# First weight tiles converted inside the attention prologue, and a new order of the two weight matrices

## The chip, the cores and the metric

The kernel runs on one core of one Trainium2 chip. The metric is the device time of one execution in microseconds (us), lower is better. Engines are named as in the profile: PE (matmul, with PEld for its weight loads), DVE (VectorE), ACT (ScalarE), POOL (GpSimd) and SP (SyncE, which only issues transfers here).

## The reference, cut to what matters

Three stages follow each other: a decaying linear attention, a feed-forward block with softplus, and a second one with a clipped gate. The weights come as float64 and all results are float32.

```python
for t in range(S):                                   # B=2, H=8, S=768, D=64
    state = gamma[None, :, None, None] * state + np.einsum('bhd,bhe->bhde', k[:, :, t], v[:, :, t])
    y[:, :, t] = scale * np.einsum('bhd,bhde->bhe', q[:, :, t], state)
x = y.transpose(0, 2, 1, 3).reshape(B * S, H * D)    # 1536 x 512
h = x @ w_in                                         # 512 x 2048
x = (np.maximum(h, 0.0) + np.log1p(np.exp(-np.abs(h)))) @ w_out
h = x @ w2_in
out = (h * np.clip(h + 3.0, 0.0, 6.0) / 6.0) @ w2_out
```

## The kernel before

**Attention** is cut into 12 units of 128 positions (two batches of six). For a unit `u`, `prepare` transposes k and q on PE and copies them out on ACT (`kT`, `qT`), and scales v (`vs`); `scores` multiplies them on PE and DVE masks the result into `pt`; `carry` multiplies q with the running state `bd` on PE, after which POOL fades `bd`; `intra` multiplies `pt` with `vs` on PE, DVE scales the sum into `on`, ACT copies it to `x_hi` and POOL subtracts to get `x_lo`; `state` adds to `bd` on DVE. Four units fill one chunk of 512 rows of x.

**The feed-forward blocks** run over three chunks of 512 rows and 16 slices `f` of the hidden width. One step is `gemm1` (12 matmuls of 128x512 on `x_hi`, `x_lo` and the two parts of a tile of w_in, then `g`, `e`, `hi` and `lo` on ACT and DVE) and, two steps later, `gemm2` (12 matmuls with a tile of w_out). Each product of float32 numbers is made of three products of shorter parts, high and low.

**Weights** arrive as pairs of 32-bit words. `fetch` loads a tile of 512 KB into one of three `raw` buffers by SP. `convert` makes the high and the low part: ACT scales the upper word, DVE clamps (`raw<-raw`), shifts (`w<-raw`) and joins in two operations of three operands (`w<-raw,w`), ACT copies out the high part, and the low part is `w` minus the high part. In the first eight conversions that subtraction is a POOL instruction (`w_parts<-w,w_parts`); in the later ones it is an accumulating transfer issued by POOL (`w_parts<-w`). The list `order` says which tile comes when: `EARLY` = 4 tiles of w_in, then w_out and w_in by turns. `feed(n)` converts up to the n-th tile; `first(f)` is the n that is called for after `gemm1` of step f in the first chunk.

**What sets the order.** While `nc.on` is true, every instruction keeps the order in which it is written, on every engine; this holds for the constants, units 0 to 3 with the preparation of unit 4, and the first two conversions (`feed(2)`, after unit 3). From then on a scheduler places what is written: units 4 to 11 are interleaved with steps 0 to 7 of the first chunk.

Of the kernel before, what the change touches and what calls it, by code (L numbers as in the profile page):

```python
# [10 lines left out]
F32 = mybir.dt.float32  # L11
# [3 lines left out]
ALU = mybir.AluOpType  # L15
# [25 lines left out]
@with_exitstack  # L41
def kernel(ctx, tc, q, k, v, w1_in, w1_out, w2_in, w2_out, tq, tk, tc_, tg, out):
    nc = InOrder(tc)
    B, H, S, D = q.shape
    NT, DM = out.shape
    DFF = w1_in.shape[1]
    NP = H // 2
    KD = DM // P
    NF = DFF // P
    C = P  # L50
    NCH = S // C
    CH = 512
    chunks1 = [(0, 0, 512), (1, 0, 512), (2, 0, 512)]
    chunks2 = [(0, 0, 512), (1, 0, 512), (2, 0, 512)]
    LAG = 2
    EARLY = 4

    tc.nc.scalar.preload_act_table_set("softplus")

    xpool = ctx.enter_context(tc.tile_pool(name="xpool", bufs=1))  # L60
    x_hi = [xpool.tile([P, KD, CH], F32R, name=f"x_hi{c}") for c in range(NT // CH)]
    x_lo = [xpool.tile([P, KD, CH], F32R, name=f"x_lo{c}") for c in range(NT // CH)]

    win_p = ctx.enter_context(tc.tile_pool(name="win", bufs=NF))
    wout_p = ctx.enter_context(tc.tile_pool(name="wout", bufs=NF))
    psum = ctx.enter_context(tc.tile_pool(name="psum", bufs=1, space=PSUM))
    raw_p = ctx.enter_context(tc.tile_pool(name="raw", bufs=3))
    cv_p = ctx.enter_context(tc.tile_pool(name="cv", bufs=2))

    w_in_t, w_out_t, raws = {}, {}, {}  # L70
    words = {0: (w1_in.bitcast(U32), w1_out.bitcast(U32)), 1: (w2_in.bitcast(U32), w2_out.bitcast(U32))}

    def fetch(m, o, f):
        raw = raw_p.tile([P, CH, 2], U32, tag="raw", name="raw")
        src = words[m][o]
        if o:
            nc.sync.dma_start(out=raw.rearrange("p n t -> p (n t)"), in_=src[f * P:(f + 1) * P, :])
        else:
            nc.sync.dma_start(out=raw.rearrange("p (k n) t -> p k (n t)", k=KD),
                              in_=src[:, 2 * f * P:2 * (f + 1) * P].rearrange("(k p) f -> p k f", p=P))  # L80
        raws[m, o, f] = raw

    def convert(m, o, f):

        raw = raws.pop((m, o, f))
        low, y = raw[:, :, 0], raw[:, :, 1]

        w = cv_p.tile([P, CH], U32, tag="w", name="w")
        nc.scalar.activation(y.bitcast(F32), y.bitcast(F32), AF.Copy, scale=2.0 ** -112)
        nc.vector.tensor_scalar(y.bitcast(F32), y.bitcast(F32), -TOP, TOP, ALU.max, ALU.min)  # L90
        nc.vector.tensor_scalar(w, y, 3, None, ALU.logical_shift_left)
        nc.vector.scalar_tensor_tensor(w, y, 0x80000000, w, ALU.bitwise_and, ALU.bitwise_or)
        nc.vector.scalar_tensor_tensor(w, low, 29, w, ALU.logical_shift_right, ALU.bitwise_or)
        t = (wout_p if o else win_p).tile([P, 2, CH], F32R, tag="w", name="w_parts")
        if done[1] < 2 * EARLY:
            nc.scalar.activation(t[:, 0], w.bitcast(F32), AF.Copy)
            nc.gpsimd.tensor_tensor(t[:, 1], w.bitcast(F32), t[:, 0].bitcast(F32), ALU.subtract)
        else:
            nc.scalar.activation(t[:, 1], w.bitcast(F32), AF.Copy, scale=-1.0)
            nc.gpsimd.dma_start(out=t[:, 1].bitcast(F32), in_=w.bitcast(F32), accum_op=ALU.add)  # L100
            nc.scalar.activation(t[:, 0], w.bitcast(F32), AF.Copy)
        if o:
            w_out_t[m, f] = t
        else:
            w_in_t[m, f] = t.rearrange("p a (k n) -> p a k n", k=KD)

    NU = B * NCH
    order = [(0, 0, f) for f in range(EARLY)]
    for f in range(NF):
        order += [(0, 1, f)] + [(0, 0, f + EARLY)] * (f + EARLY < NF)  # L110
    order += [(1, 0, f) for f in range(NF)] + [(1, 1, f) for f in range(NF)]
    done = [0, 0]

    def fetch_weights(n):
        while done[0] < min(len(order), n):
            fetch(*order[done[0]])
            done[0] += 1

    def feed(n):

        n = min(n, len(order))
        while done[1] < n:
            fetch_weights(done[1] + (1 if nc.on else 2))
            convert(*order[done[1]])
            done[1] += 1

    banks = psum.tile([P, 8, CH], F32, name="banks")
    free = list(range(8))

    def bank(hold=False):  # L130

        i = free.pop(0)
        if not hold:
            free.append(i)
            return banks[:, i, :]
        return i, banks[:, i, :]

    def release(i):
        free.append(i)

    def first(f):
        return EARLY + 2 * (f + 1) - max(0, f + 1 + EARLY - NF)

    step, last, n_steps = moe(ctx, tc, nc, out, x_hi, x_lo, w_in_t, w_out_t, chunks1, chunks2, NF, KD, DM, CH, LAG, feed, first, bank, release)
    s = 0
    with ExitStack() as actx:
        unit = attention(actx, tc, nc, q, k, v, tq, tk, tc_, tg, x_hi, x_lo, CH, bank, feed, fetch_weights)
        for u in range(CH // P, NU):
            begin, end = unit(u)
            begin()  # L150
            step(s, True, False)
            end()
            step(s, False, True)
            s += 1
    while s < n_steps:
        step(s)
        s += 1


def attention(ctx, tc, nc, q, k, v, tq, tk, tcc, tg, x_hi, x_lo, CH, bank, feed, fetch_weights):  # L160
# [4 lines left out]
    START = CH // C  # L165
# [5 lines left out]
    def ps(*shape):  # L171
        return bank().rearrange("p (a b) -> p a b", a=shape[0])
# [14 lines left out]
    def fetch(u, *which, parts=1):  # L187
        b, i = units[u]
        for nm in which:
            t = ld.tile([P, H, D], F32, tag=nm + "0" * (u < START), name=nm, bufs=START if u < START else 3)  # L190
            src = {"q": q, "k": k, "v": v}[nm][b, :, i * C:(i + 1) * C, :].rearrange("h s d -> s h d")
            for j in range(parts):
                hs = slice(j * H // parts, (j + 1) * H // parts)
                nc.sync.dma_start(out=t[:, hs], in_=src[:, hs])
            nat[nm, u] = t
# [27 lines left out]
    def carry(u):  # L223
        b, i = units[u]
        qT = tr["q", u]
        o = ps(NP, C)
        tr["o", u] = o
        if i > 0:
            for p in range(NP):
                nc.tensor.matmul(o[:, p, :], bd[b][:, p, :], qT[:, p, :], start=(p == 0), stop=False, skip_group_check=True)  # L230
        fade(u)

    def intra(u):
        b, i = units[u]
        vs, pt, o = tr["vs", u], tr["pt", u], tr["o", u]
        for h in range(H):
            g = h % 2
            nc.tensor.matmul(o[g * D:(g + 1) * D, h // 2, :], vs[:, h, :], pt[:, g, h // 2, :],
                             start=(i == 0 and h < 2), stop=True, skip_group_check=True)
        c, at = divmod(u * C, CH)  # L240
        hi, lo = x_hi[c][:, :, at:at + C], x_lo[c][:, :, at:at + C]
        on = wk.tile([P, NP, C], F32, tag="on" + "0" * (u < START), name="on", bufs=2)
        nc.vector.tensor_tensor(on, o, tq_sb, ALU.mult)
        nc.scalar.activation(hi, on, AF.Copy)
        nc.gpsimd.tensor_tensor(lo, on, hi.bitcast(F32), ALU.subtract)
# [18 lines left out]
    def fade(u):  # L264
        b, i = units[u]
        if i == 0 or i == NCH - 1:
            return
        for j in range(2):
            r = slice(j * D, (j + 1) * D)
            s = bd[b][r, :, r]  # L270
            nc.gpsimd.tensor_tensor(s, s, tc_sb[r].rearrange("p (n o) -> p n o", o=1).to_broadcast([D, NP, D]), ALU.mult)
# [12 lines left out]
    fetch(1, "v")  # L284
    for u in range(2, START):
        fetch(u, "k", "q", "v")
    fetch_weights(1)
    fetch(START, "k", "q", "v")

    def prepare(u):  # L290
        transposed(u, "k")
        transposed(u, "q")
        decayed(u)
# [9 lines left out]
    for u in range(START):  # L303
        scores(u)
        prepare(u + 1)
        carry(u)
        intra(u)
        state(u)
    feed(2)
    nc.on = False  # L310
    for u in range(START + 1, START + 3):
        fetch(u, "k", "q", "v")

    def unit(u):

# [146 lines left out]
```

## Time and profile before

| | before |
|---|---|
| median of 3 timed runs | 617.2 us (616.24 to 618.05) |
| span of the profiled execution, first to last instruction | 613.8 us |
| PE busy | 598.1 us, 97% |
| DVE busy | 351.8 us, 57% |
| ACT busy | 275.9 us, 45% |
| POOL busy | 103.4 us, 17% |

The page gives no time of the profiled execution other than its span; the timed runs lie 2.4 to 4.3 us above that span. The averages hide two stages: in the first 160 us attention, weights and the first chunk overlap and DVE is full; in most of the rest PE alone is full. So the table is read together with windows of the trace.

### The profile page before, as it was taken

The page shows a single profiled execution, that of the slowest core. Times are in us where ns is not written, and L with a number is a line of the kernel's source. Part 1 is how long each engine was busy: PE and PEld are TensorE (multiplying, and loading weights), DVE is VectorE, ACT ScalarE, POOL GpSimd, SP SyncE. Part 2 cuts the span into 40 slices and gives each one's busy share as a digit, 9 for nine tenths or more (in the row PEclk, how much of TensorE's full clock was granted, in tenths as well). Part 3 has the DMA queues.
Part 4 walks back from the last instruction along what each step waited for, and adds up shares of the span by engine and source line. Part 5 has one row for each costly group of instructions (what it writes and reads, how often), then busy time and mean ns, then how long its engine had stood idle before and what let it go on. Part 6 is the DMA issues. An engine that isn't in the chain of part 4 may idle for free.

```text
span 613.8 us, 7743 instructions
## 1 busy us (share of the span) xinstructions
PE 598.1 (97%) x2963; PEld 491.2 (80%) x2963; DVE 351.8 (57%) x583; ACT 275.9 (45%) x473; POOL 103.4 (17%) x110
## 2 busy tenths in 40 slices
PE   7988999999999999999999999999999999999997
PEld 6865778788788888888887878888888888888886
DVE  4589999999773334376667798832322222322223
ACT  3355475678563333465556687722222222222220
POOL 1745664432100000011111122200000000000000
PEclk9998999999999999999999999999999999999999
DMA  9998888799600000045566689600100000100001
GB/s 193 236 229 211 219 197 208 192 217 227 159 32 0 1 0 1 9 111 119 140 180 154 162 208 262 125 7 1 68 1 0 1 1 0 70 1 1 0 1 69
DMA packets 69510, 61.60 MB, mean 100 GB/s; under 512 B 40032, under 2 KB 56672, under 8 KB 69472
## 3 DMA queue, kind: packets, MB, share of 16 engines
q1 hardware_dynamic: 61408, 46.42, 26.6%
q0 software_dynamic: 8064, 14.68, 14.6%
q8 instruction: 23, 0.38, 0.3%
q14 instruction: 15, 0.12, 0.1%
HBM read 43.26 MB, written 3.15 MB: 76 GB/s over the span
## 4 chain that ended last, share of the span: by engine, by line
PE 66%; DVE 13%; issue 7%; DMA 6%; ACT 3%; POOL 2%; SPq 1%; DVEq 0%; POOLq 0%; ACTq 0%
PE banks L31 66%; DVE w L31 6%; DMA raw<-in_moe_w_in_dram 3%; DVE raw L31 2%; POOL w_parts L31 2%; DMA w_parts<-w 2%; DVE g L31 1%; SPq L31 1%; DVE pt L31 1%; DMA q<-in_q_dram 1%; DVE lo L31 1%; ACT e L31 1%; DVE e L31 1%; ACT raw L31 1%; ACT w_parts L31 1%
## 5 line engine op out<-in xcount | busy, mean ns | idle before, releaser
L31 PE MATMUL banks<-x_hi,w_parts 128*128 128x512 f32 x768 | 253.9, 391 | 2.4 <-POOL w_parts L31 1.2
L31 PEld LDWEIGHTS banks<-x_hi,w_parts 128*128 128x128 f32 x768 | 143.8, 188 | 34.4 <-POOL w_parts L31 2.1
L31 PE MATMUL banks<-x_lo,w_parts 128*128 128x512 f32 x384 | 149.6, 390 | 0.0
L31 PE MATMUL banks<-hi,w_parts 128*128 128x512 f32 x384 | 129.4, 397 | 0.9 <-POOL w_parts L31 0.8
L31 PE MATMUL banks<-w_parts,hi 128*128 128x512 f32 (+1 forms) x386 | 118.4, 388 | 0.7 <-DVE g L31 0.7
L31 DVE SCALAR_TENSOR_TENSOR g<-e,banks 128x512 f32<-128x512 f32 x48 | 33.0, 687 | 123.3 <-ACT e L31 123.3
L31 DVE SCALAR_TENSOR_TENSOR w<-raw,w 128x512 uint32<-128x512 uint32 x128 | 94.3, 738 | 1.6
L31 DVE TENSOR_TENSOR lo<-g,hi 128x512 fp32r<-128x512 f32 x96 | 66.3, 690 | 48.9 <-ACT hi L31 48.6
L31 POOL DMA_DIRECT2D w_parts<-w x56 | 49.3, 880 | 251.9 <-DVE e L31 98.7
L31 ACT ACTIVATE hi<-g 128x512 fp32r<-128x512 f32 x96 | 60.5, 630 | 65.0 <-DVE g L31 61.6
L31 ACT ACTIVATE e<-banks,three 128x512 f32<-128x512 f32 x48 | 32.9, 686 | 125.7 <-PE banks L31 125.7
L31 ACT ACTIVATE w_parts<-w 128x512 fp32r<-128x512 f32 x120 | 70.4, 625 | 39.2 <-DVE w L31 39.0
L31 PEld LDWEIGHTS banks<-hi,w_parts 128*128 128x128 f32 x384 | 72.8, 190 | 17.6 <-POOL w_parts L31 1.5
L31 PEld LDWEIGHTS banks<-w_parts,hi 128*128 128x128 f32 x386 | 72.3, 188 | 16.0 <-DVE g L31 1.1
L31 PEld LDWEIGHTS banks<-x_lo,w_parts 128*128 128x128 f32 x384 | 72.1, 188 | 14.9
L31 PE MATMUL banks<-lo,w_parts 128*128 128x512 f32 x192 | 75.6, 394 | 0.4 <-DVE lo L31 0.4
L31 PE MATMUL banks<-w_parts,lo 128*128 128x512 f32 (+1 forms) x193 | 74.9, 388 | 0.0
L31 DVE SCALAR_TENSOR_TENSOR e<-g,banks 128x512 f32<-128x512 f32 x48 | 32.7, 682 | 27.5 <-ACT g L31 27.5
L31 DVE TENSOR_TENSOR g<-g,e 128x512 f32<-128x512 f32 x48 | 34.4, 717 | 23.9 <-ACT e L31 23.5
L31 ACT ACTIVATE raw<-raw 128x512 f32<-128x512 f32 x64 | 42.2, 669 | 12.7 <-DMA raw<-in_moe_w_in_dram 12.7
L31 ACT ACTIVATE g<-banks 128x512 f32<-128x512 f32 x48 | 28.2, 587 | 36.5 <-PE banks L31 36.5
L31 PEld LDWEIGHTS banks<-lo,w_parts 128*128 128x128 f32 x192 | 36.5, 190 | 8.9 <-DVE lo L31 1.5
(45 smaller groups left out, 401.1 us busy)
## 6 DMA issues: line engine op xcount, KB each, us to landing
raw<-in_moe_w_in_dram SPq DMA_DIRECT2D x32, 512.0 KB, 4.2
raw<-in_moe_w_out_dram SPq DMA_DIRECT2D x32, 512.0 KB, 4.6
w_parts<-w POOLq DMA_DIRECT2D x56, 256.0 KB, 4.9
q<-in_q_dram SPq DMA_DIRECT2D x12, 256.0 KB, 5.3
v<-in_v_dram SPq DMA_DIRECT2D x12, 256.0 KB, 4.9
k<-in_k_dram SPq DMA_DIRECT2D x11, 256.0 KB, 5.3
out_dram<-ob SPq DMA_DIRECT2D x11, 256.0 KB, 2.0
k<-in_k_dram SPq DMA_DIRECT2D x2, 128.0 KB, 2.8
```

What stands on the lines that cost most here:

```text
L31: ins = getattr(self.engine, op)(*args, **kwargs)
```

## The change

Six edits go together.

- `EARLY` falls from 4 to 3: w_out and w_in alternate from the fourth tile on. `first(f)` now calls for 4 + 2f tiles after step f instead of 6 + 2f.
- `ON_DVE` = 4: the first four low parts are subtracted on DVE. `ON_POOL` = 8: the next four on POOL as before, the rest by the accumulating transfer as before.
- The first tile is fetched ahead of unit 3's k, q and v, the second ahead of unit 4's, the third ahead of unit 5's. SP issues in this order, so these loads move back by one, two and three tiles.
- `feed(u - 1)` stands inside the loop over the first units: the first conversion lies between `carry` and `intra` of unit 2, the second between those of unit 3.
- After the loop the fourth tile is fetched, ahead of unit 6.
- A fetch never looks past the end of `order`.

```diff
-    EARLY = 4
+    EARLY = 3
+    ON_DVE, ON_POOL = 4, 8
...
-        if done[1] < 2 * EARLY:
+        if done[1] < ON_POOL:
             nc.scalar.activation(t[:, 0], w.bitcast(F32), AF.Copy)
-            nc.gpsimd.tensor_tensor(t[:, 1], w.bitcast(F32), t[:, 0].bitcast(F32), ALU.subtract)
+            (nc.vector if done[1] < ON_DVE else nc.gpsimd).tensor_tensor(t[:, 1], w.bitcast(F32), t[:, 0].bitcast(F32), ALU.subtract)
...
-            fetch_weights(done[1] + (1 if nc.on else 2))
+            fetch_weights(min(len(order), done[1] + (1 if nc.on else 2)))
...
-        return EARLY + 2 * (f + 1) - max(0, f + 1 + EARLY - NF)
+        return EARLY + 2 * f + 1 - max(0, f + EARLY - NF)
...
     for u in range(2, START):
         fetch(u, "k", "q", "v")
-    fetch_weights(1)
+        fetch_weights(u - 1)
     fetch(START, "k", "q", "v")
+    fetch_weights(3)
+    fetch(START + 1, "k", "q", "v")
...
         carry(u)
+        if u >= 2:
+            feed(u - 1)
         intra(u)
         state(u)
-    feed(2)
     nc.on = False
-    for u in range(START + 1, START + 3):
-        fetch(u, "k", "q", "v")
+    fetch_weights(4)
+    fetch(START + 2, "k", "q", "v")
```

On DVE, from the masked scores of unit 2 to those of unit 4, the order was this (`pt`, `on` and `bd` belong to attention; `raw` and `w` to a conversion):

```order
L31 TENSOR_TENSOR pt<-banks,tm_sb 128x512 x2
L31 TENSOR_TENSOR on<-banks,tq_sb 128x512
L31 TENSOR_TENSOR bd_112<-bd_112,banks 64x4x64 x2
L31 TENSOR_TENSOR pt<-banks,tm_sb 128x512 x2
L31 TENSOR_TENSOR on<-banks,tq_sb 128x512
L31 TENSOR_TENSOR bd_112<-bd_112,banks 64x4x64 x2
L31 TENSOR_SCALAR raw<-raw 128x512
L31 TENSOR_SCALAR w<-raw 128x512
L31 TENSOR_TENSOR pt<-banks,tm_sb 128x512
```

and is now this, behind the masked scores of unit 2:

```order
L31 TENSOR_SCALAR raw_143<-raw_143 128x512
L31 TENSOR_SCALAR w_321<-raw_143 128x512
L31 SCALAR_TENSOR_TENSOR w_321<-raw_143,w_321 128x512 x2
L31 TENSOR_TENSOR w_parts_327<-w_321,w_parts_327 128x512
L31 TENSOR_TENSOR on_338<-banks_80,tq_sb_106 128x512
L31 TENSOR_TENSOR bd0_112<-bd0_112,banks_80 64x4x64 x2
L31 TENSOR_TENSOR pt_348<-banks_80,tm_sb_108 128x512 x2
```

and, right behind that, in unit 3:

```order
L31 TENSOR_SCALAR raw_151<-raw_151 128x512
L31 TENSOR_SCALAR w_379<-raw_151 128x512
L31 TENSOR_SCALAR raw_159<-raw_159 128x512
L31 SCALAR_TENSOR_TENSOR w_379<-raw_151,w_379 128x512
L31 TENSOR_SCALAR w_453<-raw_159 128x512
L31 SCALAR_TENSOR_TENSOR w_379<-raw_151,w_379 128x512
L31 SCALAR_TENSOR_TENSOR w_453<-raw_159,w_453 128x512
L31 TENSOR_TENSOR pt_414<-banks_80,tm_sb_108 128x512
L31 TENSOR_TENSOR w_parts_385<-w_379,w_parts_385 128x512
L31 TENSOR_TENSOR on_396<-banks_80,tq_sb_106 128x512
```

A whole conversion with its subtraction now stands ahead of `on` of unit 2, and the second one, with most of the third, ahead of `on` of unit 3.

On PE, around the first matmul with a weight tile (`w_parts`), the order was this (`qT,bd0` is `carry`, `pt,vs` is `intra`, `vs,k` is `state`, `ident` a transpose):

```order
L31 MATMUL banks_80<-qT_350,bd0_112 128x128 x4
L31 MATMUL banks_80<-pt_410,vs_352 64x128
L31 MATMUL banks_80<-vs_352,k_151 128x128 x4
L31 MATMUL banks_80<-ident_101,k_398 128x128
L31 MATMUL banks_80<-pt_410,vs_352 64x128 x7
L31 MATMUL banks_80<-ident_101,k_398 128x128 x3
L31 MATMUL banks_80<-ident_101,q_400 128x128
L31 MATMUL banks_80<-x_hi0_59,w_parts_384 128x512
L31 MATMUL banks_80<-x_lo0_62,w_parts_384 128x512
```

and is now this:

```order
L31 MATMUL banks_80<-qT_369,kT_363 128x128 x7
L31 MATMUL banks_80<-vs_371,k_153 128x128 x4
L31 MATMUL banks_80<-ident_101,k_161 128x128 x4
L31 MATMUL banks_80<-ident_101,q_163 128x128 x4
L31 MATMUL banks_80<-x_hi0_59,w_parts_327 128x512
L31 MATMUL banks_80<-qT_369,bd0_112 128x128 x2
L31 MATMUL banks_80<-x_lo0_62,w_parts_327 128x512
```

`carry` and `intra` of unit 4 stood ahead of the first weight matmul; now they stand inside and behind that step.

On PE, at unit 8 (step 4 of the first chunk), the scores `qT,kT` stood in two halves inside weight matmuls:

```order
L31 MATMUL banks<-x_hi_59,w_parts 128x512
L31 MATMUL banks<-qT,kT 128x128 x4
L31 MATMUL banks<-x_hi_59,w_parts 128x512
L31 MATMUL banks<-x_lo_62,w_parts 128x512
L31 MATMUL banks<-x_hi_59,w_parts 128x512
L31 MATMUL banks<-hi,w_parts 128x512
L31 MATMUL banks<-lo,w_parts 128x512
L31 MATMUL banks<-hi,w_parts 128x512 x2
L31 MATMUL banks<-lo,w_parts 128x512
L31 MATMUL banks<-qT,kT 128x128 x4
L31 MATMUL banks<-qT,bd_113 128x128 x4
```

and stand there in one piece now:

```order
L31 MATMUL banks<-hi,w_parts 128x512
L31 MATMUL banks<-qT,kT 128x128 x8
L31 MATMUL banks<-x_hi_59,w_parts 128x512
L31 MATMUL banks<-x_lo_62,w_parts 128x512
L31 MATMUL banks<-x_hi_59,w_parts 128x512 x2
```

Before, the scores of units 7, 8 and 9 were in halves; now only those of unit 7 are. Behind unit 11 the order of steps on PE is the same in both.

## Rows read from the trace of the kernel before

**Rows 1.** Windows: stretch, busy us (instructions) by engine, granted PE clock, DMA share, GB/s

```profile
17.40:28.97 11.57, 11.57 (x131) 10.25 (x129) 6.48 (x12) 4.64 (x8) 8.76 (x11) 1.00 1.06 245
28.97:82.80 53.83, 48.64 (x300) 37.00 (x299) 50.19 (x79) 29.05 (x53) 30.97 (x24) 0.94 0.90 225
82.80:118.52 35.72, 33.28 (x238) 27.20 (x239) 35.04 (x57) 22.45 (x42) 18.61 (x19) 1.00 0.74 179
118.52:160.00 41.48, 41.48 (x198) 34.36 (x197) 38.32 (x71) 32.37 (x59) 12.79 (x14) 1.00 0.93 217
```

The columns are PE, PEld, DVE, ACT, POOL, then clock, DMA and GB/s.

**Rows 2.** Timeline of DVE, 17 to 35 us: start, us, operation [idle before, releaser]

```profile
18.82 1.29 DVE L31 TENSOR_TENSOR pt<-banks,tm_sb 128x512 f32<-128x512 f32 x2
21.83 0.69 DVE L31 TENSOR_TENSOR on<-banks,tq_sb 128x512 f32<-128x512 f32 x1 [1.73 <-issue]
```

**Rows 3.** Timeline of ACT, 20 to 42 us

```profile
19.96 0.59 ACT L31 ACTIVATE qT<-banks 128x512 f32<-128x512 f32 x1
...
28.21 0.67 ACT L31 ACTIVATE raw<-raw 128x512 f32<-128x512 f32 x1
33.34 0.63 ACT L31 ACTIVATE w_parts<-w 128x512 fp32r<-128x512 f32 x1 [4.45 <-DVE w L31]
```

**Rows 4.** Groups of DVE by shape, 28.97 to 118.5 us: count, busy us, mean ns

```profile
L31 DVE SCALAR_TENSOR_TENSOR w<-raw,w 128x512 uint32<-128x512 uint32 x39 | 33.1, 853 | 0.3
L31 DVE TENSOR_SCALAR raw<-raw 128x512 f32<-128x512 f32 x21 | 12.2, 594 | 1.4 <-ACT raw L31 1.4
L31 DVE TENSOR_SCALAR w<-raw 128x512 uint32<-128x512 uint32 x20 | 12.0, 605 | 0.7 <-DVE raw L31 0.5
...
L31 DVE TENSOR_TENSOR lo<-g,hi 128x512 fp32r<-128x512 f32 x7 | 4.8, 679 | 0.0
```

**Rows 5.** The same view, 290 to 350 us, where POOL only issues transfers

```profile
L31 DVE SCALAR_TENSOR_TENSOR w<-raw,w 128x512 uint32<-128x512 uint32 x21 | 14.4, 688 | 0.3
...
L31 DVE TENSOR_SCALAR raw<-raw 128x512 f32<-128x512 f32 x10 | 4.3, 425 | 2.0 <-ACT raw L31 2.0
L31 DVE TENSOR_SCALAR w<-raw 128x512 uint32<-128x512 uint32 x10 | 4.2, 421 | 0.0
```

**Rows 6.** Tile w_parts, 28 to 70 us: POOL's subtractions, ns min/median/max, first and last start

```profile
L31 POOL TENSOR_TENSOR w_parts<-w,w_parts x8: 1286/1536/2201, 34.1 to 68.2; 128x512 fp32r<-128x512 f32 x8
```

**Rows 7.** Waits of DVE, 28.97 to 118.5 us: total us, times, longest

```profile
DVE raw L31 <- ACT raw L31: 1.4, 1, 1.4
DVE g L31 <- ACT e L31: 1.3, 2, 1.1
```

**Rows 8.** Timeline of DVE, 118 to 120.5 us: masked scores of unit 11

```profile
117.92 1.29 DVE L31 TENSOR_TENSOR pt<-banks,tm_sb 128x512 f32<-128x512 f32 x2
```

**Rows 9.** Timeline of PE, at six places between 34 and 159 us

```profile
34.24 0.47 PE L31 MATMUL banks<-x_hi,w_parts 128*128 128x512 f32 x1
...
59.18 1.97 PE L31 MATMUL banks<-pt,vs 128*64 128x128 f32 x14
...
68.48 1.16 PE L31 MATMUL banks<-qT,kT 64*128 64x128 f32 x8
...
102.09 1.26 PE L31 MATMUL banks<-qT,kT 64*128 64x128 f32 x16 [0.63 <-ACT qT L31]
...
119.18 1.16 PE L31 MATMUL banks<-pt,vs 128*64 128x128 f32 x16
...
158.51 0.39 PE L31 MATMUL banks<-hi,w_parts 128*128 128x512 f32 x1
```

**Rows 10.** Timeline of POOL, 146 to 153 us: a transfer that makes a low part

```profile
149.63 0.86 POOL L31 DMA_DIRECT2D w_parts<-w  x1 [2.07 <-ACT w_parts L31]
```

**Rows 11.** Page, part 6: transfers issued, KB each, median us from issue to landing

```profile
w_parts<-w POOLq DMA_DIRECT2D x56, 256.0 KB, 4.9
```

**Rows 12.** Page, part 2: granted PE clock in 40 slices of 15.3 us, in tenths

```profile
PEclk9998999999999999999999999999999999999999
```

## The prediction

> **What bounds the kernel now.** I read the windows first. From 118.5 us on PE is busy in all of its 41.48 us [rows 1], and behind unit 11 the change leaves PE's order of steps as it was. So the end moves by as much as unit 11 moves: the reader needs to know when its masked scores leave DVE (117.92 us, [rows 8]) and when PE takes them (119.18, [rows 9]). Between 28.97 and 118.52 DVE is the fuller engine: it idles 53.83 - 50.19 = 3.64 us in one window and 35.72 - 35.04 = 0.68 us in the next, PE 5.19 and 2.44 us. Between 17.40 and 28.97, in units 2 and 3, it is the other way round: PE has no idle time and DVE idles 11.57 - 6.48 = 5.09 us [rows 1]. So I take DVE's time up to 117.92 as the account to be made, and look afterwards at whether PE follows. Before 17.4 us nothing is moved.
>
> The weight tiles themselves are not what the end waits for. A late accumulating transfer, issued at 149.63, lands by the median of 4.9 us at about 154.5, and PE uses that tile at 158.51 [rows 9 to 11]: 4 us to spare. With `first(f)` two tiles lower, tiles of w_in come later and tiles of w_out earlier in DVE's order. A shift of a few us of the whole stage does not use this spare time up, since DVE and PE shift together. I cost that edit at nothing; if the cover went, each late tile would cost what it is late.
>
> **The change on DVE, part by part.**
>
> Idle time in units 2 and 3. The first conversion needs ACT's scaling of the raw tile. Before, `qT` of unit 3 ended at 19.96 + 0.59 = 20.55 [rows 3]. Now 512 KB stand in the queue ahead of unit 3's k, q and v, at 245 GB/s [rows 1] 2.1 us; what part of this the copy of q feels no row here tells, so it is 0 to 2.1, and I take 0.8, since PE used q(3) with some time in hand (nothing waited for a load there). Then the scaling (0.67, [rows 3]) runs to about 22.0, and DVE, done with unit 2's masked scores at 18.82 + 1.29 = 20.11 [rows 2], waits 1.95. Next the subtraction waits for ACT's copy of the high part: 0.63 [rows 3] and two hand-overs of about 0.1, 0.85. In unit 3 the scaling stands behind `x_hi`, `kT` and `qT`, some 0.35. Two short waits before `bd` and `pt` of unit 2 stay, 0.55. The sum is 3.7 us against 5.09: **-1.4**. The two waits of 1.73 before `on` [rows 2] are what the conversions fill. With q late by 0 or by 2.1 this term is -2.2 to -0.1.
>
> The four subtractions. The nearest row is `lo`, the same operation on the same shape: 679 ns on DVE [rows 4]. 4 x 0.68 = **+2.7**. Queued behind them are attention's `on` and `pt`, for which ACT and PE wait.
>
> What POOL no longer does. In the stage the three conversion operations cost 853, 594 and 605 ns; at 290 to 350 us, where POOL only issues transfers, 688, 425 and 421 [rows 4, 5]. The difference is 39 x 0.165 + 21 x 0.169 + 20 x 0.184 = 13.7 us, in a stage in which POOL is busy 30.97 + 18.61 = 49.6 us [rows 1]: 0.28 us of DVE's time for each us of POOL's. Four subtractions of 1.536 us [rows 6] gone: 6.1 x 0.28 = **-1.7**. Bounds are 0 (the stalls move to POOL's next instruction) and -3.4 (each holds DVE for half a subtraction more).
>
> In the SBUF — State Buffer page of the Trainium skill, section "Who interferes with whom", the rule is that DVE and GpSimd share one pair of ports under an exclusive lock, that a DVE instruction with two SBUF inputs contends for it, and that whoever issues first keeps it for the whole instruction. The longer rows of the stage agree with that. The rule speaks against half of the edit, since the moved subtraction has two SBUF inputs itself; `lo`, which has them too, kept its 679 ns with POOL 55% busy.
>
> Idle time later. Of the 4.32 us between 28.97 and 118.52, 1.4 is one wait for ACT's scaling and 1.3 are two waits for ACT's `e` [rows 7]. The fetches now start some units earlier, so I let the first go, and half of the second, since whole scores leave PE further ahead: **-2.0**. Bounds are -4.3 (no idle time left) and +2 (see the clock, below).
>
> Sum: -1.4 + 2.7 - 1.7 - 2.0 = **-2.4 us**.
>
> **Does PE follow?** PE's first weight matmul was at 34.24 [rows 9]. Now `x_hi` of unit 3 hangs on DVE: start of the first conversion 22.05, its four operations 2.85 with some stalls, wait 0.85, subtraction 0.65, `on` 0.65, `bd` 0.85, `pt` 1.3, so 29.2; then in unit 3 the wait of 0.35, seven conversion operations at about 0.7, half of `pt`, the subtraction and `on`, so 36.4; ACT's copy 0.63 and a hand-over, so 37.2. That is 3.0 later, and `carry` and `intra` of unit 4 come behind it, some 2.0 more. Against this stand the scores: in halves they cost 2 x 1.16 (68.48, [rows 9]), whole 1.26 (102.09): 1.06 for each of units 8 and 9, 2.1. So PE has 3.0 + 2.0 - 2.1 = 2.9 us more to fit in ahead of unit 11, and has 5.19 + 2.44 = 7.6 us of idle time in that stage [rows 1], most of it waits for low parts of tiles that are now ready in time. To end 2.4 earlier it must lose 5.3 of these 7.6. I think it does, but not with much to spare.
>
> **The clock.** The granted clock has 0.94 in the window from 28.97 to 82.8 [rows 1], and the slice from 46 to 61 us shows the fall [rows 12]: a level of 1.2 GHz, at which 14 small matmuls took 1.97 where 16 take 1.16 [rows 9]. It came after waits of PE for low parts. The new wait for `x_hi` (about 34 to 37) is longer, so I expect a fall right behind it and none at 56, about as long. DVE has a backlog of conversions there, so this mostly replaces the old loss; if DVE has none, `e` of step 0 comes late and costs up to 2 us, the +2 above.
>
> **Rivals.**
>
> *No difference (chance 0.25).* The later waits stay and only -1.4 + 2.7 - 1.7 = -0.4 is left: 616.8. For it: DVE idles only 4% of that stage, and earlier input does not relieve an engine that is full. Against it: the wait for ACT's scaling is a wait for a load. Or each moved subtraction takes as long on DVE as on POOL, since a POOL instruction that runs beside it holds it up: 1.54 [rows 6] instead of 0.68, that is 4 x 0.86 = +3.4, and the sum is +1.0: 618.2. I give this second mechanism 0.10 of the 0.25; the length of `lo` [rows 4] speaks against it. (It is what the lock in the Trainium skill's SBUF — State Buffer page, "Who interferes with whom", would do here.)
>
> *Slower (0.15).* PE becomes the late engine at unit 11: its first weight matmul comes 3.0 later, unit 4 behind it, and none of the 7.6 us of waits goes. Then the end moves by +2.9: 620.1. It decides from the point at which PE's waits shrink by less than 2.9. For it: the longest new wait stands exactly there, and the clock may fall in it. Against it: the low parts for which PE waited are ready before the step begins.
>
> *Much faster (0.10).* DVE loses nearly all of its idle time and PE with it, -4.3 in place of -2.0 and the upper bound of -3.4 for POOL: -1.4 + 2.7 - 3.4 - 4.3 = -6.4, 610.8.
>
> **How the numbers follow.** The profiled execution spans 613.8; the sum gives 611.4. The median of the timed runs is 617.2, 3.4 above that span, and I carry the 3.4 over: 614.8. This case has a chance of 0.50, and its own range, from the bounds of its terms taken two at a time, is 612.5 to 616.5. The range that should hold the time 8 times in 10 reaches from 611.5 to 618.4: it takes in the case of no difference and leaves out most of the slower one and half of the much faster one. About 0.3%, 1.85 us, is what a measurement can tell from no change. Faster by more than that: 0.44 of the forecast's 0.50 and the much faster case, 0.54. Within: the rest of the forecast and 0.23 of the second case, 0.29. Slower: the third and what is left, 0.17.
>
> **What would show it.** In the changed kernel's windows DVE should idle about 3.7 us in the stretch that answers to units 2 and 3, and no weight tile should head PE's waits ahead of step 3. The first weight matmul should start near 37 us. The masked scores of unit 11 should leave DVE near 115.5 and PE be full from there on. DVE's conversion operations should have means some 3% lower than in [rows 4]. The forecast is wrong if DVE idles more than 6 us behind unit 3, if PE reaches unit 11 after its masked scores are ready, if the moved subtractions take over 1 us each, or if PE has waits for weight tiles behind unit 11.

## The result, and the profile after

The changed kernel takes 623.99 us (median of 11 runs, 621.26 to 626.15) where the kernel before takes 618.61 (11 runs beside it, 615.55 to 622.21). The ratio is 1.0098, with a 95% interval from 1.0072 to 1.0123: slower by one per cent, 5.4 us between the two medians. The forecast was 614.8, and the range ended at 618.4. The profiled execution of the changed kernel spans 619.5 us, against 613.8 before; it took 621.26, the shortest of its runs.

The windows that answer to [rows 1], with the same columns (PE, PEld, DVE, ACT, POOL, clock, DMA share, GB/s); the last line reaches to the end of unit 11's masked scores:

```profile
17.40:28.97 11.57, 9.61 (x94) 7.83 (x92) 8.73 (x15) 5.51 (x10) 6.07 (x8) 1.00 1.05 234
28.97:82.80 53.83, 47.67 (x339) 38.87 (x337) 52.19 (x79) 26.06 (x48) 25.89 (x23) 0.97 0.79 192
82.80:118.52 35.72, 30.15 (x204) 24.10 (x204) 31.89 (x51) 20.64 (x39) 17.70 (x19) 0.95 0.84 204
28.97:124.83 95.86, 83.22 (x580) 67.35 (x578) 90.33 (x139) 49.79 (x91) 45.63 (x43) 0.96 0.80 195
```

The same last stretch of the kernel before, up to the end of its unit 11:

```profile
28.97:119.20 90.23, 82.61 (x543) 64.77 (x541) 85.92 (x137) 51.50 (x93) 49.58 (x43) 0.96 0.84 208
```

Units 2 and 3 went as foreseen: DVE idles 11.57 - 8.73 = 2.84 us there, not 5.09. Up to 82.8 us the two kernels are level (from 17.40 us on PE has run 429 matmuls before, 431 after). Behind it PE falls back: between 82.80 and 118.52 it has 30.15 us of work in place of 33.28, and a clock of 0.95. At the end of unit 11 the changed kernel is 124.83 - 119.20 = 5.63 us late, and at the end of the span 5.7.

The account of DVE up to that point, from these lines and [rows 1]: before, 6.48 + 85.92 = 92.40 us busy and 9.40 idle; after, 8.73 + 90.33 = 99.06 busy and 8.37 idle. So DVE does not wait longer, it works 6.66 us longer, of which the four subtractions are 2.9 (0.69, 0.68, 0.68 and 0.81). The rest, 3.8 us, is in instructions that were there before. Its groups by shape, 28.97 to 125 us, against [rows 4] (count, busy us, mean ns, idle time before):

```profile
L31 DVE SCALAR_TENSOR_TENSOR w<-raw,w 128x512 uint32<-128x512 uint32 x38 | 31.4, 836 | 0.3
L31 DVE TENSOR_SCALAR w<-raw 128x512 uint32<-128x512 uint32 x19 | 13.0, 687 | 2.4 <-DMA w_parts<-w 2.3
L31 DVE TENSOR_SCALAR raw<-raw 128x512 f32<-128x512 f32 x20 | 11.4, 581 | 0.5 <-ACT raw L31 0.3
...
L31 DVE TENSOR_TENSOR lo<-g,hi 128x512 fp32r<-128x512 f32 x7 | 8.3, 1179 | 0.8 <-ACT hi L31 0.8
```

`lo` has gone from 679 to 1179 ns, 7 x 0.5 = 3.5 us, and the shift that makes `w` from 605 to 687. The first timeline is DVE's, the second POOL's, at three of these `lo` (start, us, operation, idle before):

```profile
52.91 1.53 DVE L31 TENSOR_TENSOR lo<-g,hi 128x512 fp32r<-128x512 f32 x1
...
64.25 1.37 DVE L31 TENSOR_TENSOR lo<-g,hi 128x512 fp32r<-128x512 f32 x1 [0.75 <-ACT hi L31]
...
76.30 1.53 DVE L31 TENSOR_TENSOR lo<-g,hi 128x512 fp32r<-128x512 f32 x1
```

```profile
52.66 1.23 POOL L31 TENSOR_TENSOR vs<-v,tk_sb 128x512 f32<-128x512 f32 x1
...
63.77 1.30 POOL L31 TENSOR_TENSOR x_lo<-on,x_hi 128x512 fp32r<-128x512 f32 x1 [3.52 <-ACT x_hi L31]
...
76.22 1.07 POOL L31 TENSOR_TENSOR vs<-v,tk_sb 128x512 f32<-128x512 f32 x1
```

Each of the three begins 0.08 to 0.5 us behind the start of a POOL instruction and takes twice its time. The two that began beside `x_lo` and beside the first `vs` end at 65.62 and 54.44, that is 0.55 us behind the end of that instruction (65.07 and 53.89), and the third ends 0.54 us behind it: most of `lo` is done only after the other has ended. Operations of one input in SBUF are longer beside POOL too: the shift here, and in [rows 4, 5] the clamp and the shift, at 594 and 605 ns against 425 and 421.

PE's waits, 82.80 to 124.83 us (total us, times, longest), and its timeline at the longest of them:

```profile
PE banks L31 <- DVE e L31: 3.6, 2, 2.8
PE banks L31 <- DVE pt L31: 1.7, 2, 1.5
```

```profile
88.81 0.66 PE L31 MATMUL banks<-ident,q 128*128 128x128 f32 x4 [2.85 <-DVE e L31]
...
89.53 0.39 PE L31 MATMUL banks<-lo,w_parts 128*128 128x512 f32 x1
...
90.34 0.63 PE L31 MATMUL banks<-lo,w_parts 128*128 128x512 f32 x1
```

DVE just before it, and behind it the line of ACT that makes the input of `e`:

```profile
83.21 0.71 DVE L31 TENSOR_SCALAR w<-raw 128x512 uint32<-128x512 uint32 x1
83.96 1.25 DVE L31 SCALAR_TENSOR_TENSOR w<-raw,w 128x512 uint32<-128x512 uint32 x1
85.13 0.83 DVE L31 TENSOR_SCALAR raw<-raw 128x512 f32<-128x512 f32 x1
85.89 1.52 DVE L31 SCALAR_TENSOR_TENSOR w<-raw,w 128x512 uint32<-128x512 uint32 x1
87.73 0.43 DVE L31 TENSOR_SCALAR w<-raw 128x512 uint32<-128x512 uint32 x1 [0.32 <-DMA w_parts<-w]
88.07 0.68 DVE L31 SCALAR_TENSOR_TENSOR e<-g,banks 128x512 f32<-128x512 f32 x1
```

```profile
83.62 0.59 ACT L31 ACTIVATE g<-banks 128x512 f32<-128x512 f32 x1
```

The transposes of `q` need the PSUM bank that `e` empties. ACT is done with `g` at 84.21, but `e` starts at 88.07: it stands behind five conversion operations, four of them drawn out. A little later the granted clock falls to 0.5, that is 1.2 GHz: the same matmul takes 0.63 in place of 0.39, from 90.1 to 93.5 us.

### The profile page after: what moved, and what is told of

The parts are those of the page before. It is cut to its first block, busy times and chain, and to the rows that moved or that the text cites. A ratio compares the mean times of both kernels' runs of the same rounds, so it can differ in the third digit from the quotient of the medians.

```text
span 619.5 us, 7735 instructions
## 1 busy us (share of the span) xinstructions
PE 596.6 (96%) x2963; PEld 491.4 (79%) x2963; DVE 359.6 (58%) x587; ACT 275.6 (44%) x473; POOL 96.2 (16%) x106
## 4 chain that ended last, share of the span: by engine, by line
PE 63%; DVE 12%; DMA 12%; issue 6%; ACT 4%; POOL 2%; SPq 1%; DVEq 0%; POOLq 0%; ACTq 0%
PE banks L31 63%; DVE w L31 6%; DMA w_parts<-w 5%; DMA raw<-in_moe_w_in_dram 4%; DMA q<-in_q_dram 2%; DVE raw L31 2%; DVE g L31 1%; DVE e L31 1%; SPq L31 1%; DVE lo L31 1%; ACT e L31 1%; ACT hi L31 1%; DMA v<-in_v_dram 1%; ACT raw L31 1%; ACT w_parts L31 1%
## 5 line engine op out<-in xcount | busy, mean ns | idle before, releaser
L31 DVE TENSOR_TENSOR lo<-g,hi 128x512 fp32r<-128x512 f32 x96 | 69.7, 726 | 49.0 <-ACT hi L31 48.8
L31 ACT ACTIVATE e<-e 128x512 f32<-128x512 f32 x48 | 30.3, 631 | 35.2 <-DVE e L31 35.1
```

The costliest lines, as they stand in the source:

```text
L31: ins = getattr(self.engine, op)(*args, **kwargs)
```

## The experiments

Each kernel was timed beside the kernel before on the same chip. The runs fall into six sets, the changed kernel's and e to i, and the kernel before has medians from 616.74 to 618.61 us in them: across sets the ratios are to be compared, not the times. The last column is where the profiled execution starts the pair of masked scores of unit 11 (117.92 before, 123.54 after); it shows whether a difference arose up to there or later. It is one execution of each kernel, and those of the kernel before lie 6 us apart (615.55 to 622.21), so a difference of 1 or 2 us in it decides nothing.

| run | median us | ratio to before, 95% | unit 11 |
|---|---|---|---|
| changed kernel | 623.99 | 1.0098 (1.0072 to 1.0123) | 123.54 |
| e1_lowparts_on_dve | 632.04 | 1.0234 (1.0212 to 1.0255) | 118.12 |
| e2_order_only | 616.43 | 0.9982 (0.9966 to 0.9998) | 118.01 |
| e3_prologue_only | 618.24 | 1.0016 (1.0002 to 1.0030) | 122.33 |
| e4_after_old_order | 637.28 | 1.0317 (1.0292 to 1.0342) | 120.63 |
| f1_after_four_w | 629.99 | 1.0205 (1.0164 to 1.0246) | 122.20 |
| f2_before_four_w | 624.93 | 1.0128 (1.0085 to 1.0172) | 123.87 |
| f3_lowparts_four_w | 634.87 | 1.0271 (1.0223 to 1.0319) | 123.97 |
| f4_before_two_w | 653.67 | 1.0588 (1.0546 to 1.0631) | 131.04 |
| g1_after_subs_on_pool | 613.86 | 0.9954 (0.9935 to 0.9972) | 116.20 |
| g2_order_and_lowparts | 632.46 | 1.0255 (1.0220 to 1.0290) | 116.06 |
| g3_lowparts_three_w | 636.91 | 1.0332 (1.0289 to 1.0376) | 119.50 |
| g4_after_three_w | 640.43 | 1.0381 (1.0342 to 1.0420) | 126.14 |
| h1_after_swapped | 618.36 | 1.0021 (1.0000 to 1.0043) | 120.37 |
| h2_before_swapped | 616.42 | 0.9987 (0.9963 to 1.0012) | 118.38 |
| h3_after_no_subs_swapped | 615.44 | 0.9979 (0.9958 to 1.0000) | 115.88 |
| h4_after_two_subs | 624.70 | 1.0128 (1.0095 to 1.0161) | 125.47 |
| i1_after_no_decay | 612.22 | 0.9896 (0.9857 to 0.9934) | 115.08 |
| i2_before_no_decay | 613.31 | 0.9925 (0.9889 to 0.9961) | 116.56 |

### The parts alone

My first theory was that the new tile order costs the time. PE's program order in units 8 to 11 had become a strict sequence (scores, first product, carry, intra, state, transposes, second product), where before it had halves of the scores and pieces of other steps between these. The rivals: VectorE is full, and four subtractions more are simply late; or the new prologue costs it.

e1 is the kernel before, with:

```diff
+    ON_DVE = 4
-            nc.gpsimd.tensor_tensor(t[:, 1], ...)
+            (nc.vector if done[1] < ON_DVE else nc.gpsimd).tensor_tensor(t[:, 1], ...)
```

> The kernel before, with only the first four low parts subtracted on VectorE. Order theory (the time is lost in units 8 to 11, where the tile order with EARLY = 3 and the new first() leave PE no matmuls between a state product and the next transposes): this edit alone moves nothing much, 617 to 620 us, with PE's order in units 8 to 11 near that of before. Full-DVE theory (four subtractions of 0.68 us more on an engine that is full, 2.7 us, and nothing saved elsewhere): 621 or more.

e2 is the kernel before, with:

```diff
-    EARLY = 4
+    EARLY = 3
-        return EARLY + 2 * (f + 1) - max(0, f + 1 + EARLY - NF)
+        return EARLY + 2 * f + 1 - max(0, f + EARLY - NF)
```

> The kernel before, with only EARLY = 3 and the new first(): the matrices alternate from the fourth tile, everything else stays. Order theory: nearly all of the loss, 622 to 625 us, PE waiting for VectorE's e and pt between 85 and 112 us, a second fall of the clock there, and the second masked score of unit 10 some 5 us later than 105.84. Full-DVE theory: no loss, 616 to 619.5.

e3 is the changed kernel with `EARLY = 4`, the old `first` and `ON_DVE = 0`; e4 is the changed kernel with the first two of these.

> The kernel before, with only the fetches among the attention loads and the conversions in units 2 and 3; all low parts on GpSimd, EARLY = 4 and the old first(). Order theory: 615 to 619 us, unit 11 no later than before (118.5 us or earlier). Full-DVE theory: 617 to 620, since nothing is added to VectorE. Prologue theory (the later first weight matmul and the wait near 34 us are what costs): 621 or more.

> The changed kernel with EARLY = 4 and the old first(): prologue and low parts as changed, order of tiles as before. Order theory: the loss is gone, 614.5 to 618.5 us, PE's order in units 8 to 11 with halves of the scores and pieces of other steps spread among them again. Full-DVE and prologue theories: the loss stays, 622 to 625.

The order alone costs nothing (616.43), so my first theory fell. The prologue alone costs at most 0.3%, though in its one trace unit 11 is 4.4 us late. e1 and e4 took 632 and 637 us, more than the whole change, and at unit 11 e1 is only 0.2 us late. So the parts do not add up to the whole. The loss of e1 lies behind 300 us, in the conversions of layer 2. Windows of e1, columns as above, and the wait of its DVE between 300 and 420 us:

```profile
300.00:350.00 50.00, 46.38 (x194) 35.59 (x193) 32.29 (x56) 27.19 (x50) 6.99 (x8) 1.00 0.59 142
350.00:400.00 50.00, 43.63 (x182) 34.65 (x181) 35.05 (x67) 30.26 (x54) 10.56 (x12) 0.93 0.71 179
```

```profile
DVE w L31 <- DMA w_parts<-w: 21.8, 13, 4.4
```

The kernel before has 1.7 us of this wait there and the changed kernel 1.6; PE is busy 49.67 and 49.31 us of these two windows before, 50.00 and 49.42 after. So four instructions in the first 60 us put 9 us of waiting into a stage 250 us behind them, while DVE's and PE's work there is the same. It cannot be their work.

### The buffer of the word tile

A new wait for these transfers stands in the changed kernel up to unit 11 too (2.3 us, in the groups above). The packer that chooses the addresses gave `w` four in turn in units 4 to 11 before, three after; and two in turn in layer 2 of e1 and e4 (no view here shows addresses). I tried buffers of my own, the same edit on three kernels, with R = 4, and R = 2 on the kernel before:

```diff
-    cv_p = ctx.enter_context(tc.tile_pool(name="cv", bufs=2))
+    cv_p = ctx.enter_context(tc.tile_pool(name="cv", bufs=1))
+    ring = [cv_p.tile([P, CH], U32, name=f"w{i}") for i in range(R)]
-        w = cv_p.tile([P, CH], U32, tag="w", name="w")
+        w = ring[done[1] % len(ring)]
```

> The changed kernel with four fixed buffers for the word tile w, used in turn, where before the packer chose its addresses (three in turn in units 4 to 11 of the changed kernel, four in turn there in the kernel before). Buffer theory (VectorE's next w waits for the accumulating transfer that still reads the same bytes, e and pt stand behind it, PE behind them): 615 to 619.5 us, no wait of VectorE for that transfer between 82 and 126 us and unit 11's second masked score back near 119. Crowding theory (the four subtractions and the new order together are what delays e and pt): it stays at 622 to 626.

> The kernel before with the same four fixed buffers for w. Buffer theory: 614 to 618 us, about the kernel before, which has four in turn up to unit 11 and three later. Crowding theory: the same. It is the partner of the run on the changed kernel with four fixed buffers.

> The kernel before, with only the four low parts on VectorE, and four fixed buffers for w. Without the fixed buffers it took 632 us, with only two addresses for w in turn behind the sixth us of layer 2's conversions. Buffer theory: 616 to 621 us, PE without waits between 300 and 400 us. Crowding theory: 628 or more.

> The kernel before with two fixed buffers for w: the reverse dose. Buffer theory: each conversion waits for the transfer two tiles back, as long as that reaches into it; between 300 and 400 us alone that cost the low-parts kernel some 10 us, so 630 us or more. Crowding theory: 616 to 620, since nothing is added to VectorE.

f1, f2 and f4 were slower than their partners, and f3 is no faster than e1: the buffer theory's forecast came true for f4 alone, the crowding theory's for f3 alone. In f1 DVE's wait for the transfer up to unit 11 falls from 2.3 to 0.4 us and unit 11 comes 1.3 us earlier; so this wait is worth a quarter of the 5.6 or so, as far as one trace tells. Then f1 loses in layer 2: its PE has 93.06 us of work done between 300 and 400 us, the changed kernel's 99.42. And f2 is 6 us late at unit 11 with as many addresses up to there as the kernel before; its trace is of the longest of its runs, 2.9 us above their median. Two buffers cost 37 us, so too little room is dear, but more room did not save time.

### Two parts together

g1 is the changed kernel with `ON_DVE = 0`. g2 is e2 with the edit of e1. g3 is e1, and g4 the changed kernel, with

```diff
-    cv_p = ctx.enter_context(tc.tile_pool(name="cv", bufs=2))
+    cv_p = ctx.enter_context(tc.tile_pool(name="cv", bufs=3))
```

> The changed kernel with all low parts on GpSimd again (new prologue and new order kept). VectorE-account theory (unit 11 is late by the four subtractions, 2.7 us, and by longer VectorE instructions beside GpSimd, 3.9 us, less idle time): without the subtractions unit 11's second masked score starts 2 to 4 us before 124.15, and the time is 619 to 622 us. Prologue-and-order theory (these two clash): it stays at 622 to 626. Its w addresses in layer 2 rotate over three, so nothing is expected to be lost between 290 and 345 us.

> The kernel before with EARLY = 3, the new first() and the four low parts on VectorE; the prologue as before. VectorE-account theory: unit 11's second masked score within 1.5 us of 118.5, since order alone moved it by 0.1 and the low parts alone by 0.2. Layer-2 theory (two addresses in turn for w in layer 2, as in the two kernels that lost some 10 us between 290 and 345 us): it has these two addresses as well, and should lose there again, 628 to 634 us; if the addresses don't matter, 616 to 619.

> The kernel before with the four low parts on VectorE and a pool of three for w in place of two; in layer 2 its w addresses rotate over three. Layer-2 theory: the loss of some 10 us between 290 and 345 us that the same edit had with two is gone, 616 to 620 us. If the low parts themselves cost that loss: 628 or more.

> The changed kernel with a pool of three for w in place of two. Its addresses rotate over three throughout, as they already do up to unit 11 of the changed kernel. Buffer theory for units 8 to 11 (VectorE waits 2.3 us for transfers that still read w): no gain, 621 to 626. VectorE-account theory: the same order of size; a gain of more than 3 us would speak against both.

g1 is the fastest version that computes everything: 613.86 us, 2.9 below the kernel before and, by the ratios, 1.4% or some 9 us below the changed one. Its windows:

```profile
17.40:28.97 11.57, 11.10 (x116) 9.39 (x114) 9.64 (x16) 5.73 (x10) 7.62 (x8) 1.00 1.03 245
28.97:117.49 88.52, 78.22 (x551) 63.54 (x551) 83.95 (x131) 49.42 (x88) 48.60 (x44) 0.96 0.83 201
```

Prologue and order together are worth having; the four subtractions on VectorE undo it. But 9 us for 2.7 us of work needed a reason, and g2 has the same four subtractions and reaches unit 11 1.9 us earlier than the kernel before. g3 refutes the two addresses alone as the cause in layer 2: with three in turn DVE's wait for the transfers from 300 to 420 us falls from 21.8 to 12.7, and still as much is lost there (PE busy 43.85 of the 50 us behind 300). g4, for which both theories had some 621 to 626 us, took 640.43: most of its loss is the same one (PE has 90.61 us of work done between 300 and 400 us, the changed kernel 99.42, and DVE waits 13.1 us for transfers from 300 to 420, not 1.6). What sets off the waits of layer 2 stays open; that they need no change of work in that stage is shown by e1.

### The same work in another order

A scheduler orders each engine's instructions anew after every edit. From g1 to the changed kernel, the subtractions themselves left out of the count, 123 of the first 200 DVE instructions stand at another place in the trace. The question was whether the work or this order costs the 9 us. h1, h2 and h3 are the changed kernel, the kernel before and g1 with one pair of independent steps written the other way round, in the units from 4 on:

```diff
-            state(u)
             if u + 1 < len(units):
                 prepare(u + 1)
+            state(u)
```

> The changed kernel with two independent steps written the other way round from unit 4 on: the transposes and the decay for the next unit ahead of the state product of this one. No work is added or left out. Work theory (the changed kernel is late because VectorE has four more subtractions): 622 to 626 us as without the swap. Order theory (what counts is the static order that the scheduler makes anew after each edit): away from 624 by 2 us or more, to either side.

> The kernel before with the same swap of two independent steps from unit 4 on, no work added or left out. Work theory: 616 to 619 us. Order theory: away from 617 by 2 us or more, to either side.

> The changed kernel with all low parts on GpSimd (613.9 us) and the same swap. Work theory: 612 to 616 us. Order theory: away from 614 by 2 us or more, to either side; then the gain of that version isn't one of its work either.

h4 is the changed kernel with `ON_DVE = 2`. Of PE's first 800 matmuls in the traces, which reach to some 125 us, 55 stand elsewhere than in the changed kernel, against 177 in h1 and 250 in g1. (The first 200 end at 24 us, ahead of unit 4, and are the same in all of these.) On DVE, though, it is 101 of the first 200, against 77 in h1.

> The changed kernel with two of the four low parts on VectorE instead of four (the two that are converted in units 2 and 3). Work theory: half way between 613.9 (none) and 624 (four), 617 to 621 us. Order theory: no such step; its order in the first 200 instructions of TensorE is nearly that of the changed kernel (7 moved, by at most 2), so near 624 if that order is what costs, with unit 11 some 4 to 6 us late and the clock falling again near 90 us.

h1 takes 618.36 us: 5.6 less than the changed kernel with the same instructions, 4.7 by the ratios. The two profiled executions lie 3.8 us apart (spans of 619.5 and 615.7), and 3.2 of this is there at unit 11. Its windows, and PE's wait for `e` from 82.80 to the end of unit 11:

```profile
82.80:118.52 35.72, 32.90 (x248) 27.13 (x246) 33.39 (x57) 23.74 (x43) 18.60 (x19) 1.00 0.89 220
...
28.97:121.65 92.68, 80.70 (x570) 65.74 (x570) 87.57 (x137) 50.41 (x91) 45.55 (x43) 0.94 0.81 197
```

```profile
PE banks L31 <- DVE e L31: 2.8, 3, 1.7
```

Between 82.80 and 118.52 the clock stays at 1.00 where the changed kernel had 0.95, and PE has 32.90 us of work done, not 30.15; h1's own falls of the clock lie ahead of that. h4, with half the added work, gains nothing (624.70), against the work theory; it has nearly the changed kernel's order on PE, but not on DVE. So the order theory holds for this difference: one and the same work takes 4 to 5 us less. It does not hold everywhere. For h2 and h3 it had forecast 2 us or more, and the swap was worth 0.3 us in the kernel before and cost 1.6 in g1. And between h1 and h3, where the swap is in both, the four subtractions cost 618.36 - 615.44 = 2.9 us, near their own time; as the orders of h1 and h3 differ too, that match is not a proof.

### One GpSimd instruction less

Last, the instructions that grew. i1 is the changed kernel, i2 the kernel before, each with the decay of `v` left out from unit 4 on:

```diff
     def decayed(u):
+        if u >= START:
+            tr["vs", u] = nat["v", u]
+            return
```

> The changed kernel with the multiplication that decays v on GpSimd left out from unit 4 on (v is used as it is). Holding theory (a VectorE instruction with two inputs in SBUF that meets a GpSimd instruction stays until that ends; lo does so 4 times of 7 in the changed kernel, three of them beside this multiplication or the x_lo behind it): lo falls from a median of 1.37 us towards 0.68, and VectorE's busy time up to unit 11 by 3 us or more. If lo's length has another reason, its median stays near 1.37.

> The kernel before with the same multiplication left out from unit 4 on. Holding theory: the conversion operations of VectorE fall below their means of 838, 627 and 588 ns between 29 and 119 us. If their length has another reason, they stay.

The tile `lo` on DVE, ns as min/median/max with first and last start: the kernel before, the changed one, and i1:

```profile
L31 DVE TENSOR_TENSOR lo<-g,hi x7: 675/678/685, 44.5 to 114.9; 128x512 fp32r<-128x512 f32 x7
```

```profile
L31 DVE TENSOR_TENSOR lo<-g,hi x7: 680/1374/1764, 45.9 to 118.5; 128x512 fp32r<-128x512 f32 x7
```

```profile
L31 DVE TENSOR_TENSOR lo<-g,hi x7: 677/685/1812, 43.7 to 112.4; 128x512 fp32r<-128x512 f32 x7
```

The window of i1 up to the end of its unit 11:

```profile
28.97:116.37 87.40, 79.47 (x577) 64.83 (x578) 85.40 (x140) 51.09 (x92) 34.45 (x35) 1.00 0.89 215
```

Without eight multiplications of 1.2 us on POOL the changed kernel takes 612.22, by the ratios 2.0% or some 12 us less. The median of `lo` is back at 0.69, DVE is busy 5 us less up to unit 11 (8.60 + 85.40 = 94.00 against 99.06), and the clock does not fall. In i2 the three conversion operations come down by 25, 35 and 16 ns only and DVE's busy time up to unit 11 by 0.4 us (6.50 + 85.49 = 91.99), yet the time by 5 us, 1.8 between the profiled executions: there the holding of DVE is not what was gained, and what was stays open. So POOL's instructions do hold DVE's. But what is held is not yet lost. These are h2's window up to the end of unit 11, and `lo` in h2 and in h1:

```profile
28.97:119.67 90.70, 79.98 (x535) 62.31 (x534) 88.57 (x136) 52.28 (x94) 50.93 (x44) 0.98 0.82 204
```

```profile
L31 DVE TENSOR_TENSOR lo<-g,hi 128x512 fp32r<-128x512 f32 x7 | 8.4, 1202 | 0.1
```

```profile
L31 DVE TENSOR_TENSOR lo<-g,hi 128x512 fp32r<-128x512 f32 x7 | 8.4, 1197 | 0.1
```

In h2 `lo` takes as long as in the changed kernel and DVE is busy 6.79 + 88.57 = 95.36 us, 3.0 more than before, with no subtraction added; unit 11 is only 0.5 us later, since DVE idles 2.5 us less, and the time is the same. In h1 `lo` takes as long too, and the 2.9 us that DVE is less busy than in the changed kernel (96.13 against 99.06) are in the conversions. So the length of `lo` is a mark of the meetings and not the loss itself. That the static order decides which instructions meet, and whether `e` and `pt` are late by it, is the reading that fits h1 and i1 together. But i1 has a new order as well, and its PE has no `vs` to wait for; no run keeps the order and moves a meeting alone, so this is argued and not shown.

## Why the prediction was wrong, point by point

**DVE's idle time in units 2 and 3, -1.4:** right in kind, small in size. It is 2.84 us, 2.25 less than before. The two waits that I priced stand in the trace, at 1.42 for 1.95 and 0.70 for 0.85:

```profile
21.37 0.78 DVE L31 TENSOR_SCALAR raw<-raw 128x512 f32<-128x512 f32 x1 [1.42 <-ACT raw L31]
...
25.05 0.69 DVE L31 TENSOR_TENSOR w_parts<-w,w_parts 128x512 fp32r<-128x512 f32 x1 [0.70 <-ACT w_parts L31]
```

**Four subtractions, +2.7:** right. They take 0.69, 0.68, 0.68 and 0.81 us, 2.9 together, and h1 against h3 has 2.9 us at the end.

**Saved contention, -1.7, and its bound at 0:** the first step that failed. I made one rate (0.28 us of DVE for each us of POOL) and took it to fall with POOL's busy time. POOL's time fell, from 8.76 + 49.58 to 6.07 + 45.63 us, and DVE's longer instructions cost 3.8 us more. `lo` "kept its 679 ns with POOL 55% busy" was my evidence against the Trainium skill's rule (SBUF — State Buffer, "Who interferes with whom") that a DVE instruction with two SBUF inputs contends and whoever issues first holds the ports. It was luck of place: six of the seven `lo` of the kernel before had no POOL instruction under way as they began, and the seventh began 0.01 us behind one. The trace after agrees with the rule, at 1.37 to 1.76 us for four of seven `lo`. The price is one of meetings, and its sign can't be read from POOL's share. My rival of 0.10, in which a POOL instruction holds up what runs beside it on DVE, had the mechanism but at the subtractions, which hardly grew; it fell on `lo` and the shift.

**Idle time later, -2.0:** failed. Behind 28.97 us DVE idles 95.86 - 90.33 = 5.53 us against 4.31. The waits that I let go did go (ACT's `e`, most of ACT's scaling), and others came: 2.3 us for the accumulating transfers, which no row of before had shown as a price, and 0.8 and 0.7 for ACT's `hi` and PE's scores. With what was measured the sum is -2.25 + 2.9 + 3.8 + 1.2 = 5.6 us, which is what unit 11 is late; the two terms with which I had -3.7 came to +5.0.

**The order, "I cost that edit at nothing":** alone it did cost nothing (e2). What failed stands beside it: "DVE and PE shift together", and the scores in one piece as a pure gain of 2.1. The block of steps did not shift, it was dealt anew; with fewer foreign matmuls between state and transposes, PE had nothing to do while `e` was late. h1 and the changed kernel show 4 to 5 us between two orders of one and the same work; that it is this lack of foreign matmuls is argued, as e2 has the new order of tiles and no loss.

**PE's first weight matmul, 37.2:** right. It is at 36.72, behind the wait that I placed between 34 and 37:

```profile
36.06 0.66 PE L31 MATMUL banks<-ident,q 128*128 128x128 f32 x4 [2.24 <-DVE on L31]
36.72 0.50 PE L31 MATMUL banks<-x_hi,w_parts 128*128 128x512 f32 x1
```

And no matmul waits for a weight tile afterwards, as I said; three weight loads wait for ACT's high parts, 1.1 us in all. **"It must lose 5.3 of these 7.6"** was the weak point. I had misread those 7.6 us as mostly waits for low parts; the kernel before has this much of them, from 28.97 to 119.20:

```profile
PE banks L31 <- POOL w_parts L31: 2.0, 3, 0.8
```

They went, and so little was to be had from them. I named the point as the slower rival: its point of decision was that PE's waits shrink by less than 2.9. They grew: in 28.97 to 124.83 PE is not busy for 12.64 us, against 7.62 before. The rival's price, +2.9 and 620.1, was too small, since the waits did not only stay, and its place was wrong: not at the first weight matmul alone but also at `pt` and `e` in units 6 to 10, the longest 3.36 us at 57.71.

**The clock:** no fall came right behind the wait at 34 to 37, as I had expected one. There are two, of 3.4 us each, from 59.4 and from 90.1 us, each behind a wait of PE for DVE; before there was one of 6.8 us from 56.2. In the two profiled executions the clock is level (a mean of 0.994 after, 0.993 before), and 5.7 us lie between them all the same. In most other runs of the changed kernel it is lower (median 0.986; the kernel before, in the runs beside e1 to e4, 0.996), which adds to the time of those runs.

**The signs that I had named** told it well: unit 11's masked scores at 123.54 instead of near 115.5, the shift's mean up instead of 3% down. In the swapped order the same change costs 618.36 - 616.42 = 1.9 us, so the forecast of -2.4 would have missed there as well; the other 3.5 of the 5.4 us go with the order. And my own range of 612.5 to 616.5 is not what its bounds give two at a time: it moves one term each way, and the two largest on the slow side, +4.0 and +1.7, make 620.5, still short of 623.99.

## What to carry to other kernels

Where a scheduler deals the instructions anew, a sum of parts is not a forecast: swap two independent lines first, in both kernels, and see by how much the time moves with no work changed. Here that was 0.3, 1.6 and some 5 us, as much as the change itself. On a full VectorE, look at which long instruction meets which GpSimd instruction, not at shares; and when three edits come in one change, time it without each, since the best version here (613.86 us) was the change less one of its parts.

## What the runs showed of the hardware

The holding goes both ways: in the kernel before a `lo` that began at 52.37 took its 0.68 us, and POOL's subtraction that began at 52.59 took 2.20 instead of 1.29 at the least [rows 6]. Leaving one multiplication of 1.2 us in each of eight units out on GpSimd, with the new order that comes of it, took some 12 us off the changed kernel and 5 off the kernel before. And a transfer that adds into SBUF holds the tile that it reads for some 5 us [rows 11]; with two buffers for that tile the whole kernel took 653.67 us.
